# Moving parts of the last layer's bias to ScalarE and dropping one summand from TensorE in a six-layer cross network

## The chip, the cores and the metric

The kernel runs on one core of a Trainium2 chip. The metric is the device time of one execution in microseconds, the median over several executions. The engines that matter here are TensorE (PE in the profile, its weight loads PEld), VectorE (DVE), ScalarE (ACT) and the issuing queues of the transfers (SPq, ACTq). All engines run side by side, each through its own instructions in order, and wait for each other through semaphores.

## The reference

```python
B, F, D, L = 4096, 26, 16, 6
Din = min(F * D, 1024)          # 416
# x0: (4096, 416), ws: (6, 416, 416), bs: (6, 416), all bf16

def reference(x0, ws, bs):
    x = x0
    for l in range(ws.shape[0]):
        x = x0 * (x @ ws[l] + bs[l]) + x
    return x
```

Since every layer multiplies by the same x0, the state can be written x = x0 * c, where c starts at 1 and each layer adds x @ ws[l] + bs[l] to it. The kernel keeps this c, and multiplies it by x0 to get the next layer's input.

## The kernel before

**Layout.** For the layers 0 to 4 everything is transposed: the 416 features lie on the partitions, as three main blocks of 128 (index m) and a remainder of 32, and the 4096 rows of the batch lie along the free axis, as two strips (index s) of 2048 columns, each of four groups of 512. A tile is a pair (s, m). `CM` holds c for the main blocks, `CR` for the remainder (four groups of 32 features stacked on 128 partitions, 512 columns for each strip), `XM0` and `XR[0]` hold x0, `XH` and `XR[1..]` the layer's input and output.

**Layers 1 to 3.** For each tile TensorE forms the product in PSUM in two tiles of 1024 columns (`pt`), ScalarE copies each to SBUF with the bias added (L187), VectorE adds it to c (L188) and multiplies by x0 (L189). The remainder goes through `ew_rem` (L191): ScalarE copies its 512 columns of PSUM in pieces of 256 or 128 columns (L197), then come one add and one multiply on VectorE (L203, L204). The PSUM pool has four tiles of two banks, taken in turn, so TensorE can fill a tile only when ScalarE has copied the one that lay there four tiles earlier.

**The fifth layer, `feeding_layer`** (l = 4), does the same, but it also prepares what the last layer needs of c. The last layer works in rows: its output block of 128 batch rows by 416 features is x0 * (c + b5 + x @ w5), and so c + b5 is wanted in rows. For each of the six tiles A, Bt, C (strip 0, m = 0, 1, 2) and Dt, E, F (strip 1), `rows_out` (L351) adds the last layer's bias to c in place on VectorE (L349), and a transposing transfer on the SP queue turns it into `XLrows` (L232). For strip 1 only the first three of each group's four blocks of 128 columns get the bias; the fourth belongs to the last group of output blocks, whose bias TensorE adds itself (L481). `rem_out` (L378) does the same for the remainder, by way of `scrR` (L380), and `xl_rem` (L307) copies that into `XLrows` on ScalarE (L312). Since the bias is added to c in place, the multiply that makes the last layer's input from c (L345, L376) has to be done before it.

The order of VectorE's work in this layer is written out by hand: `pin` keeps the instructions of an engine in program order. The names in that list are `evict` (ScalarE's copy out of PSUM, L333), `add` (L341), `mul` (L345; with a 4 it takes the four groups, 2048 columns, in one instruction), `rem` (L374, L376), `last_bias` (L349). `layer_products` computes two tiles and calls `between` after the products of the first: there ScalarE evicts that first tile, and for the pair E, F the function `before_last` (L408) puts `xl_rem(0)` ahead of it.

**The last layer** works through eight quads of four output blocks, two quads a round, in four rounds. In a round u counts the eight blocks; each has a PSUM bank. TensorE computes the block (L464 for the main blocks, L477 for the remainder), ScalarE copies it to a tile `t` (L519), VectorE adds `XLrows` (L523), and one step later multiplies by `X0rows` (L505, in `close_product`), and SP issues the transfer to the output (L508). The multiply of a block is queued on VectorE when the next block's add has been queued: add u, multiply u - 1, add u + 1, multiply u, and so on.

In the final round the last three blocks, u = 5, 6 and 7, get their summand c on TensorE instead (`adds`): c's block is multiplied by the identity into the same bank, three products of 128 columns and one of 32 (L468, L470). ScalarE's copies of u = 5 and 6 then need no add on VectorE, and the block u = 7 isn't copied at all: VectorE multiplies it straight out of PSUM (`direct`). The blocks 4 and 5 leave in one transfer, 6 and 7 each in one of its own, the last on ScalarE's queue.

Of the kernel before, what the change touches and what calls it, by code (L numbers as in the profile page):

```python
# [9 lines left out]
ACT = mybir.ActivationFunctionType  # L10
ALU = mybir.AluOpType
# [5 lines left out]
def kernel(  # L17
# [7 lines left out]
    nc = tc.nc  # L25
    B, D = x0.shape
    L = ws.shape[0]
    P = 128
# [5 lines left out]
    CW = 512  # L34
    SW = NG * CW
    NBT = B // P
    LL = L - 1
# [18 lines left out]
    bM = const.tile([P, NK, L], FP32)  # L56
    bR = const.tile([P, L], FP32)
# [9 lines left out]
    CM = big.tile([P, NK, B], BF16, name="CM")  # L67
    CR = big.tile([P, NS * CW], BF16, name="CR")

    def col0(s, g):  # L70
        return SW * s + CW * g
# [8 lines left out]
    def pin(ins):  # L80
        tc.keep_in_program_order(ins)
# [109 lines left out]
    def ew_rem(l, s, pr, nxtR):  # L191
        cols = slice(CW * s, CW * s + CW)
        halves = [slice(a, a + CW // 2) for a in range(0, CW, CW // 2)]
        base = CR[:, cols] if l == 0 else tpool.tile([P, 2 * CW], BF16, name="t")
        n = CW // (4 if l == 2 or l and s else 2)
        for a in range(0, CW, n):
            nc.scalar.activation(base[:, a:a + n], pr[:, a:a + n], ACT.Identity, bias=bR[:, l:l + 1], scale=1.0)  # L197
        if l == 0:
            for a in halves:
                part = slice(CW * s + a.start, CW * s + a.stop)  # L200
                pin(nc.vector.tensor_tensor(out=nxtR[:, part], in0=CR[:, part], in1=XR[0][:, part], op=ALU.mult))
            return
        nc.vector.tensor_tensor(out=CR[:, cols], in0=base[:, 0:CW], in1=CR[:, cols], op=ALU.add)  # L203
        nc.vector.tensor_tensor(out=nxtR[:, cols], in0=CR[:, cols], in1=XR[0][:, cols], op=ALU.mult)  # L204
# [102 lines left out]
    def xl_rem(s):  # L307
        dst = XLrows[:, 16 * s:16 * s + 16, NK * P:D].rearrange("p (g i) r -> p i g r", g=NG)
        src = scrR[s][:].rearrange("p i (g r) -> p i g r", g=NG)
        n = 4 if s else 2  # L310
        for i in range(0, 4, n):
            pin(nc.scalar.copy(dst[:, i:i + n], src[:, i:i + n]))  # L312
# [13 lines left out]
    def feeding_layer(l, cur, curR, nxt, nxtR):  # L326
        tiles = [(s, m) for s in range(NS) for m in range(NK)]
        pts, ts = {}, {}

        def evict(t):  # L330
            for h in range(2):
                ts[t + (h,)] = tpool.tile([P, 2 * CW], BF16, name="t")
                nc.scalar.activation(ts[t + (h,)][:], pts[t][h][:].rearrange("p a b -> p (a b)"), ACT.Identity,  # L333
                                     bias=bM[:, t[1], l:l + 1], scale=1.0)

        def c_of(t, h):
            c0 = col0(t[0], 2 * h)
            return CM[:, t[1], c0:c0 + 2 * CW]

        def add(t, h):  # L340
            pin(nc.vector.tensor_tensor(out=c_of(t, h), in0=ts[t + (h,)][:], in1=c_of(t, h), op=ALU.add))  # L341

        def mul(t, h=0, n=2):
            c0, w = col0(t[0], 2 * h), n * CW
            pin(nc.vector.tensor_tensor(out=nxt[t[0]][:, t[1], 2 * CW * h:2 * CW * h + w], in0=CM[:, t[1], c0:c0 + w],  # L345
                                        in1=XM0[:, t[1], c0:c0 + w], op=ALU.mult))

        def last_bias(c, bias):
            pin(nc.vector.tensor_scalar(out=c, in0=c, scalar1=bias, scalar2=None, op0=ALU.add))  # L349

        def rows_out(t):  # L351
            s, m = t
            c = CM[:, m, SW * s:SW * s + SW]
            if s:
                c = c.rearrange("p (g r) -> p g r", g=NG)[:, :, 0:3 * P]
            last_bias(c, bM[:, m, LL:L])
            xl_dmat(s, m)

        A, Bt, C, Dt, E, F = tiles
        layer_products(l, 0, tiles, pts, cur, curR, evict)  # L360
        evict(Bt)
        pr2 = psum.tile([P, 2, CW], FP32, tag="ps", name="pr2")
        for s in range(NS):
            mm_rem(l, s, pr2[:, s, :], cur, curR)
        tr = []
        for s in range(NS):
            tr.append(tpool.tile([P, 2 * CW], BF16, name="t"))
            for a in range(0, CW, CW // 2):
                nc.scalar.activation(tr[s][:, a:a + CW // 2], pr2[:, s, a:a + CW // 2], ACT.Identity, bias=bR[:, l:l + 1], scale=1.0)

        def rem(s, op):
            part = slice(CW * s, CW * s + CW)
            if op == ALU.add:
                pin(nc.vector.tensor_tensor(out=CR[:, part], in0=tr[s][:, 0:CW], in1=CR[:, part], op=op))  # L374
            else:
                pin(nc.vector.tensor_tensor(out=nxtR[:, part], in0=CR[:, part], in1=XR[0][:, part], op=op))  # L376

        def rem_out(s):  # L378
            last_bias(CR[:, CW * s:CW * s + (3 * P if s else CW)], bR[:, LL:L])
            nc.sync.dma_start_transpose(out=scrR[s][:], in_=CR[:, CW * s:CW * s + CW])  # L380

        add(A, 0)
        mul(A, 0)
        add(A, 1)
        add(Bt, 0)
        mul(A, 1)
        add(Bt, 1)
        rows_out(A)
        rem(0, ALU.add)
        mul(Bt, 0, 4)  # L390
        rem(0, ALU.mult)
        rem(1, ALU.add)
        rem_out(0)
        rows_out(Bt)
        rem(1, ALU.mult)

        layer_products(l, 2, tiles, pts, cur, curR, evict)
        evict(Dt)
        add(C, 0)
        add(C, 1)  # L400
        rem_out(1)
        mul(C, 0, 4)
        add(Dt, 0)
        add(Dt, 1)
        rows_out(C)
        mul(Dt, 0, 4)

        def before_last(t):  # L408
            xl_rem(0)
            evict(t)  # L410

        layer_products(l, 4, tiles, pts, cur, curR, before_last)
        evict(F)
        add(E, 0)
        rows_out(Dt)
        add(E, 1)
        mul(E, 0, 4)
        add(F, 0)
        add(F, 1)
        rows_out(E)  # L420
        mul(F, 0, 4)
        xl_rem(1)
        return lambda: rows_out(F)
# [22 lines left out]
    l = LL  # L446
# [14 lines left out]
    def mm_q_full(q, g, py, closes, adds=False):  # L461
        s, i = quads[q]
        for k in range(NK):
            nc.tensor.matmul(py[:, 0:D], lhsT=q_x(q, g, k), rhs=WM[:, l, k, :],  # L464
                             start=((not closes) and k == 0), stop=(closes and not adds and k == NK - 1))
            if adds:
                c0 = col0(s, g) + 128 * i
                nc.tensor.matmul(py[:, P * k:P * k + P], lhsT=CM[:, k, c0:c0 + 128], rhs=ident[:], start=False, stop=False)  # L468
        if adds:
            nc.tensor.matmul(py[:, NK * P:D], lhsT=CR[:, CW * s + 128 * i:CW * s + 128 * i + 128],  # L470
                             rhs=ident[:, 32 * g:32 * g + 32], start=False, stop=True)
# [59 lines left out]
    for q, at, done in rounds:  # L531
        tiles = [psum.tile([P, 2, CW], FP32, tag="ps", name=f"py{n}") for n in range(4)]
        bank = [tiles[n][:, a, :] for n, a in at]

        final = q + 2 == NQ

        def close(groups):
            u = groups[0][0]
            srcs = [tiles[at[g[0]][0]][:, at[g[0]][1]:at[g[0]][1] + len(g), 0:D] for g in groups]
            if q == 0:  # L540
                evict_quad(u, srcs[0])
                return
            paired = final and u in (0, 1, 4, 5)
            j = u % 2 if paired else 0
            if not j:
                outs.append(opool.tile([P, 2, D], BF16, name="o"))
            ew(q + u // 4, u % 4, srcs, outs[-1], j, bool(j) or not paired, nc.scalar if final and u == 7 else nc.sync,
               final and u >= 5, final and u == 7)

        for u in range(done):  # L550
            if q == 0:
                mm_q_open(q, u, bank[u])
            else:
                mm_q_full(q, u, bank[u], False)
        mm_q_rem(q, bank[0:4], done)
        close([range(done)])
        mm_q_rem(q + 1, bank[4:8], 0)
        for u in range(done, 8):
            mm_q_full(q + u // 4, u % 4, bank[u], True, final and u >= 5)
            if at is ENDS:  # L560
                close([[u]])
            elif u % 2:
                close([[u - 1, u]] if at is PAIRS else [[u - 1], [u]])
                if q == 0 and u == 3:
                    last_rows_out()
# [31 lines left out]
```

## Time and profile before

| | |
|---|---|
| median of 3 runs | 128.79 us (128.64 to 128.90) |
| the profiled execution's own time | 128.94 us |
| its span, first to last instruction | 127.1 us |
| granted TensorE clock, mean | 0.995 |
| busy: PE, DVE, ACT | 122.9, 102.4, 89.0 us |
| rate of the transfers over the span | 129 GB/s |

The profile shows one execution. What lies outside the span (128.94 - 127.1, some 1.8 us) is start and end of the program and is the same for both kernels. Rows of the timeline read: start in us from the span's start, duration, engine, line of the kernel, operation, output and inputs with their shapes, and in brackets the idle time of the engine just ahead and what ended it. A row "x4" stands for four instructions one behind the other, with the time from the start of the first to the end of the last. An instruction's duration includes a part that overlaps the next one on its engine, so in a row of instructions the distance from start to start is shorter than the duration; sums are made with that distance. "L349" is line 349 of the kernel before.

### The profile page before, as it was taken

The page shows a single profiled execution, that of the slowest core. Times are in us where ns is not written, and L with a number is a line of the kernel's source. Part 1 is how long each engine was busy: PE and PEld are TensorE (multiplying, and loading weights), DVE is VectorE, ACT ScalarE, POOL GpSimd, SP SyncE. Part 2 cuts the span into 40 slices and gives each one's busy share as a digit, 9 for nine tenths or more (in the row PEclk, how much of TensorE's full clock was granted, in tenths as well). Part 3 has the DMA queues.
Part 4 walks back from the last instruction along what each step waited for, and adds up shares of the span by engine and source line. Part 5 has one row for each costly group of instructions (what it writes and reads, how often), then busy time and mean ns, then how long its engine had stood idle before and what let it go on. Part 6 is the DMA issues. An engine that isn't in the chain of part 4 may idle for free.

```text
span 127.1 us, 3940 instructions
## 1 busy us (share of the span) xinstructions
PE 122.9 (97%) x1682; PEld 55.2 (43%) x1682; DVE 102.4 (81%) x188; ACT 89.0 (70%) x117; POOL 4.6 (4%) x18
## 2 busy tenths in 40 slices
PE   7999999999999999999999999999999999999990
PEld 3243443453444354435344535443534445455450
DVE  0023679774989898998898998898999999999991
ACT  0137865896869486879495869495859698688770
POOL 4004000310000000000000000000000000000000
PEclk9999999999999999999999999999999999999997
DMA  3999999999990000000000000000039999999975
GB/s 93 245 219 218 164 211 241 220 329 334 337 309 26 0 5 0 8 0 5 0 5 0 5 0 0 5 0 5 0 71 140 204 72 247 186 220 329 286 251 163
DMA packets 42230, 16.38 MB, mean 129 GB/s; under 512 B 31034, under 2 KB 42212, under 8 KB 42212
## 3 DMA queue, kind: packets, MB, share of 16 engines
q1 hardware_dynamic: 37432, 15.40, 54.9%
q10 hardware_dynamic: 4780, 0.72, 3.7%
q8 instruction: 13, 0.21, 0.8%
q14 instruction: 5, 0.04, 0.1%
HBM read 6.15 MB, written 3.41 MB: 75 GB/s over the span
## 4 chain that ended last, share of the span: by engine, by line
PE 68%; DVE 17%; DMA 8%; issue 3%; ACT 1%; DVEq 1%
PE pt L209 40%; PE ph L241 13%; DMA XLrows<-CM 8%; PE wps L148 4%; PE pt L215 4%; PE pr L225 4%; DVE XH L345 4%; DVE CM L341 4%; DVE o L505 3%; DVE t L523 3%; PE ph L248 2%; DVE CM L349 1%; PE pr L221 1%; ACT t L333 1%; DVE CR L374 1%
## 5 line engine op out<-in xcount | busy, mean ns | idle before, releaser
L209 PE MATMUL pt<-XH,WM 128*32 128x512 bf16 x1152 | 65.2, 379 | 0.0
L187 ACT ACTIVATE t<-pt,bM 128x1024 bf16<-128x1024 f32 x36 | 37.2, 1115 | 12.5 <-PE pt L215 12.5
L209 PEld LDWEIGHTS <-WM 128*32 128x32 bf16 x1152 | 29.7, 97 | 33.8 <-issue 5.1
L188 DVE TENSOR_TENSOR CM<-t,CM 128x1024 bf16<-128x1024 bf16 x36 | 24.7, 686 | 4.3 <-ACT t L187 4.3
L189 DVE TENSOR_TENSOR XH<-CM,XM 128x1024 bf16<-128x1024 bf16 x36 | 24.9, 692 | 2.6
L464 PE MATMUL py<-WM,XH 128*128 128x416 bf16 x90 | 17.0, 339 | 0.0
L241 PE MATMUL ph<-XM,WM 128*128 128x512 bf16 x72 | 16.4, 380 | 0.0
L333 ACT ACTIVATE t<-pt,bM 128x1024 bf16<-128x1024 f32 x12 | 12.4, 1115 | 4.1 <-PE pt L215 4.1
L181 ACT ACTIVATE CM<-ph,bM 128x1024 bf16<-128x1024 f32 x12 | 12.5, 1113 | 3.5 <-PE ph L248 3.5
L519 ACT CAST t<-py 128x416 bf16<-128x416 f32 (+1 forms) x18 | 10.8, 602 | 3.2 <-PE py L464 1.4
L183 DVE TENSOR_TENSOR XH<-CM,XM 128x512 bf16<-128x512 bf16 x24 | 8.9, 432 | 4.1 <-ACT CM L181 4.0
L464 PEld LDWEIGHTS <-XH 128*128 128x128 bf16 x90 | 8.5, 98 | 7.5 <-issue 1.2
L241 PEld LDWEIGHTS <-WM 128*128 128x128 bf16 x72 | 6.7, 98 | 8.4 <-issue 1.1
L341 DVE TENSOR_TENSOR CM<-t,CM 128x1024 bf16<-128x1024 bf16 x12 | 8.0, 687 | 0.3 <-ACT t L333 0.3
L345 DVE TENSOR_TENSOR XH<-CM,XM 128x2048 bf16<-128x2048 bf16 (+1 forms) x7 | 7.5, 1068 | 0.2
L215 PE MATMUL pt<-XR,WR 32*128 32x512 bf16 x96 | 7.3, 379 | 0.0
L505 DVE TENSOR_TENSOR o<-t,X0rows 128x832 bf16<-128x832 bf16 (+1 forms) x15 | 7.1, 482 | 0.0
L197 ACT ACTIVATE t<-pr,bR 128x128 bf16<-128x128 f32 (+1 forms) x20 | 5.9, 400 | 1.6 <-PE pr L225 1.6
L225 PE MATMUL pr<-XH,WM 128*32 128x512 bf16 x96 | 6.6, 379 | 0.0
L523 DVE TENSOR_TENSOR t<-t,XLrows 128x832 bf16<-128x832 bf16 (+1 forms) x13 | 6.5, 500 | 0.0
L114 ACT ACT_TABLE_LOAD x1 | 1.3, 1283 | 6.0 <-DMA XM<-in_x_dram 6.0
L157 DVE CAST bM<-pb 128x18 f32<-128x18 bf16 x1 | 0.2, 177 | 5.6 <-PE pb L156 5.6
(64 smaller groups left out, 69.2 us busy)
## 6 DMA issues: line engine op xcount, KB each, us to landing
X0rows<-in_x_dram SPq DMA_DIRECT2D x15, 208.0 KB, 4.9
out_dram<-o SPq DMA_DIRECT2D x10, 208.0 KB, 3.4
WM<-in_ws_dram SPq DMA_DIRECT2D x5, 312.0 KB, 5.8
out_dram<-XH SPq DMA_DIRECT2D x4, 208.0 KB, 3.3
WR<-in_ws_dram SPq DMA_DIRECT2D x4, 130.0 KB, 5.3
WM<-in_ws_dram ACTq DMA_DIRECT2D x1, 312.0 KB, 3.2
out_dram<-o SPq DMA_DIRECT2D x3, 104.0 KB, 1.9
X0rows<-in_x_dram SPq DMA_DIRECT2D x2, 104.0 KB, 5.1
```

The costliest lines, as they stand in the source:

```text
L181: nc.scalar.activation(c, src, ACT.Identity, bias=bias, scale=1.0)
L187: nc.scalar.activation(t[:], src, ACT.Identity, bias=bias, scale=1.0)
L188: nc.vector.tensor_tensor(out=c, in0=t[:], in1=c, op=ALU.add)
L189: nc.vector.tensor_tensor(out=x, in0=c, in1=XM0[:, m, c0:c0 + 2 * CW], op=ALU.mult)
L209: nc.tensor.matmul(pts[g // 2][32 * q:32 * q + 32, g % 2, :], lhsT=WM[:, l, k, 128 * m + 32 * q:128 * m + 32 * q + 32], rhs=cur[s][:, k, C ...
L215: nc.tensor.matmul(pts[g // 2][:, g % 2, :], lhsT=WR[32 * g:32 * g + 32, l, 128 * m:128 * m + 128], rhs=curR[32 * g:32 * g + 32, CW * s:CW ...
L225: nc.tensor.matmul(pr[32 * g:32 * g + 32, :], lhsT=WM[:, l, k, NK * P:D], rhs=cur[s][:, k, CW * g:CW * g + CW], start=False, stop=(k == NK ...
L241: nc.tensor.matmul(pt[:, gl, :], lhsT=WM[:, 0, k, 128 * m:128 * m + 128], rhs=cur[:, k, c0:c0 + CW], start=(k == 0 and not after_row), sto ...
L333: nc.scalar.activation(ts[t + (h,)][:], pts[t][h][:].rearrange("p a b -> p (a b)"), ACT.Identity, bias=bM[:, t[1], l:l + 1], scale=1.0)
L341: pin(nc.vector.tensor_tensor(out=c_of(t, h), in0=ts[t + (h,)][:], in1=c_of(t, h), op=ALU.add))
L345: pin(nc.vector.tensor_tensor(out=nxt[t[0]][:, t[1], 2 * CW * h:2 * CW * h + w], in0=CM[:, t[1], c0:c0 + w], in1=XM0[:, t[1], c0:c0 + w], ...
L464: nc.tensor.matmul(py[:, 0:D], lhsT=q_x(q, g, k), rhs=WM[:, l, k, :], start=((not closes) and k == 0), stop=(closes and not adds and k == ...
```

## The change

Five edits:

- In `ew_rem` the remainder of strip 1 in layer 3 is copied in two pieces of 256 columns instead of four of 128. Layers 1 and 2 stay as they are.
- The last bias of the remainder of strip 0 goes from VectorE to ScalarE (`rem_bias(0)`, 512 columns), and the multiply `rem(0, ALU.mult)` is moved ahead of `mul(Bt, 0, 4)` so that the bias can follow it at once. The bias of strip 1's remainder stays on VectorE, but is moved from behind `add(C, 1)` to ahead of it, with its transfer.
- Of tile C's last bias, ScalarE adds the upper 1024 of 2048 columns (`half_bias`), VectorE the lower 1024 (`rows_out(C, True)`). `half_bias` stands in `before_last`, on ScalarE between `xl_rem(0)` and the eviction of E.
- `rows_out(Dt)` is moved from behind `add(E, 0)` to ahead of it.
- In the final round block 5 gets its summand on VectorE like the blocks before it; TensorE adds it for the blocks 6 and 7 alone.

What is computed is the same.

```diff
@@ -192,7 +192,7 @@
         cols = slice(CW * s, CW * s + CW)
         halves = [slice(a, a + CW // 2) for a in range(0, CW, CW // 2)]
         base = CR[:, cols] if l == 0 else tpool.tile([P, 2 * CW], BF16, name="t")
-        n = CW // (4 if l == 2 or l and s else 2)
+        n = CW // (4 if l == 2 or (s and l == 1) else 2)
         for a in range(0, CW, n):
             nc.scalar.activation(base[:, a:a + n], pr[:, a:a + n], ACT.Identity, bias=bR[:, l:l + 1], scale=1.0)
         if l == 0:
@@ -348,9 +348,14 @@
         def last_bias(c, bias):
             pin(nc.vector.tensor_scalar(out=c, in0=c, scalar1=bias, scalar2=None, op0=ALU.add))
 
-        def rows_out(t):
+        def half_bias(t):
             s, m = t
-            c = CM[:, m, SW * s:SW * s + SW]
+            c = CM[:, m, SW * s + 2 * CW:SW * s + SW]
+            pin(nc.scalar.activation(c, c, ACT.Identity, bias=bM[:, m, LL:L], scale=1.0))
+
+        def rows_out(t, done=False):
+            s, m = t
+            c = CM[:, m, SW * s:SW * s + (2 * CW if done else SW)]
             if s:
                 c = c.rearrange("p (g r) -> p g r", g=NG)[:, :, 0:3 * P]
             last_bias(c, bM[:, m, LL:L])
@@ -375,8 +380,14 @@
             else:
                 pin(nc.vector.tensor_tensor(out=nxtR[:, part], in0=CR[:, part], in1=XR[0][:, part], op=op))
 
+        def rem_bias(s):
+            c = CR[:, CW * s:CW * s + (3 * P if s else CW)]
+            if s:
+                last_bias(c, bR[:, LL:L])
+            else:
+                pin(nc.scalar.activation(c, c, ACT.Identity, bias=bR[:, LL:L], scale=1.0))
+
         def rem_out(s):
-            last_bias(CR[:, CW * s:CW * s + (3 * P if s else CW)], bR[:, LL:L])
             nc.sync.dma_start_transpose(out=scrR[s][:], in_=CR[:, CW * s:CW * s + CW])
 
         add(A, 0)
@@ -387,8 +398,9 @@
         add(Bt, 1)
         rows_out(A)
         rem(0, ALU.add)
+        rem(0, ALU.mult)
+        rem_bias(0)
         mul(Bt, 0, 4)
-        rem(0, ALU.mult)
         rem(1, ALU.add)
         rem_out(0)
         rows_out(Bt)
@@ -397,22 +409,24 @@
         layer_products(l, 2, tiles, pts, cur, curR, evict)
         evict(Dt)
         add(C, 0)
+        rem_bias(1)
+        rem_out(1)
         add(C, 1)
-        rem_out(1)
         mul(C, 0, 4)
         add(Dt, 0)
         add(Dt, 1)
-        rows_out(C)
-        mul(Dt, 0, 4)
 
         def before_last(t):
             xl_rem(0)
+            half_bias(C)
+            rows_out(C, True)
+            mul(Dt, 0, 4)
             evict(t)
 
         layer_products(l, 4, tiles, pts, cur, curR, before_last)
         evict(F)
+        rows_out(Dt)
         add(E, 0)
-        rows_out(Dt)
         add(E, 1)
         mul(E, 0, 4)
         add(F, 0)
@@ -545,7 +559,7 @@
             if not j:
                 outs.append(opool.tile([P, 2, D], BF16, name="o"))
             ew(q + u // 4, u % 4, srcs, outs[-1], j, bool(j) or not paired, nc.scalar if final and u == 7 else nc.sync,
-               final and u >= 5, final and u == 7)
+               final and u >= 6, final and u == 7)
 
         for u in range(done):
             if q == 0:
@@ -556,7 +570,7 @@
         close([range(done)])
         mm_q_rem(q + 1, bank[4:8], 0)
         for u in range(done, 8):
-            mm_q_full(q + u // 4, u % 4, bank[u], True, final and u >= 5)
+            mm_q_full(q + u // 4, u % 4, bank[u], True, final and u >= 6)
             if at is ENDS:
                 close([[u]])
             elif u % 2:
```

## The prediction

> **What bounds the kernel now.** I read the page first: busy times and the chain of waits.
>
> ```profile
> PE 122.9 (97%) x1682; PEld 55.2 (43%) x1682; DVE 102.4 (81%) x188; ACT 89.0 (70%) x117; POOL 4.6 (4%) x18
> ...
> PE 68%; DVE 17%; DMA 8%; issue 3%; ACT 1%; DVEq 1%
> ```
>
> TensorE is never idle between the first products and the last block, so up to there nothing gets faster unless TensorE does less or is stalled less. VectorE has the next share of the chain. So next the waits of VectorE from 86 to 128 us:
>
> ```profile
> DVE CM L341 <- ACT t L333: 0.3, 1, 0.3
> ```
>
> One wait, at the first add of the fifth layer; from there VectorE runs back to back to the end and is the second bound. Then the timeline of the last 8 us; these rows are picked from it:
>
> ```profile
> 119.26 2.46 PE L464 MATMUL py<-WM,XH 128*128 128x416 bf16 x13
> ...
> 121.63 0.51 ACT L519 CAST t<-py 128x416 bf16<-128x416 f32 x1
> 122.11 0.34 PE L464 MATMUL py<-WM,XH 128*128 128x416 bf16 x1
> 122.59 0.36 DVE L505 TENSOR_TENSOR o<-t,X0rows 128x416 bf16<-128x416 bf16 x1
> 123.16 0.36 DVE L505 TENSOR_TENSOR o<-t,X0rows 128x416 bf16<-128x416 bf16 x1
> 123.52 0.18 PE L470 MATMUL py<-ident,CR 128*128 128x32 bf16 x1
> 123.56 0.38 SPq L508 DMA_DIRECT2D out_dram<-o  x1
> 123.84 0.58 DVE L505 TENSOR_TENSOR o<-py,X0rows 128x416 bf16<-128x416 f32 x1
> 124.03 0.42 SPq L508 DMA_DIRECT2D out_dram<-o  x1
> 124.46 0.38 ACTq L508 DMA_DIRECT2D out_dram<-o  x1
> ```
>
> The thirteenth of the first row's products, at 119.26 + 2.46 - 0.34 = 121.38, is the first of block 5, and 122.11 the first of block 6. 122.59 is the multiply of block 3, 123.16 that of block 5, 123.84 that of block 7. The transfer of blocks 4 and 5 is issued at 123.56, as soon as block 5's multiply ends (123.52); those of 6 and 7 follow. Last, the transfers in stretches (the last two columns are the busy share of the transfer engines and GB/s):
>
> ```profile
> 124.20:124.50 0.30, 0.00 (x0) 0.00 (x0) 0.23 (x1) 0.00 (x0) 0.00 (x0) 1.00 0.17 47
> 124.50:125.80 1.30, 0.00 (x0) 0.00 (x0) 0.00 (x0) 0.00 (x0) 0.00 (x0) 0.98 0.96 312
> ```
>
> After a gap comes one full burst, 1.30 x 312 = 406 KB, which is the last three transfers (208, 104 and 104 KB). So the end is set by the burst, and the burst begins with the transfer of blocks 4 and 5: it is released by block 5's multiply, some 0.95 us ahead of it (123.56 to 124.50). Block 7 by itself would end almost as late: 124.46 + 0.95 + 0.33 for its 104 KB is 125.74.
>
> **The change part by part.** *Final round.* TensorE loses block 5's four small products. Block 5 took 122.11 - 121.38 = 0.73; its three products of 416 columns alone take 0.53 (twelve take from 119.26 to 121.38, 0.177 each). So TensorE ends 0.20 earlier: block 7 is complete at 123.52 + 0.18 - 0.20 = 123.50. But VectorE gets an add, and it is queued ahead of the multiplies of blocks 4 to 7. Multiplies of 416 columns follow each other by 0.285 (122.59 to 123.16 is two of them). Without any help from layer five: multiply 3 at 122.59, add 5 at 122.88, multiply 4 at 123.16, 5 at 123.45, 6 at 123.73, 7 at 124.02: block 5 is 0.29 later than before, block 7 0.18. TensorE's 0.20 doesn't help, since multiply 7 waits for multiply 6 on VectorE. Had VectorE all the lead one can wish for, add 5 would still wait for its copy: ScalarE is busy with block 4 until 121.63 + 0.53, so the copy ends at 122.67 and add 5 begins at 122.69; then multiply 5 is at 123.26 (+0.10) and multiply 7 at 123.83 (-0.01).
>
> *How much lead there can be.* In rounds three and four VectorE follows ScalarE's copies closely:
>
> ```profile
> 118.20 0.51 ACT L519 CAST t<-py 128x416 bf16<-128x416 f32 x1
> 118.80 0.58 DVE L523 TENSOR_TENSOR t<-t,XLrows 128x832 bf16<-128x832 bf16 x1
> ```
>
> This copy ends at 118.71 and could release the add some 0.03 later (the hand-over from block 5's multiply to its issue, 123.52 to 123.56, is of that size), at 118.74: a lead of 0.06 at most passes here. The copies are paced by TensorE, which doesn't change before block 5. So whatever layer five saves, at most 0.06 reaches the final round.
>
> *VectorE in layer five.* Rows for the bias, for the wait between dependent instructions and for the gate at E:
>
> ```profile
> 88.53 0.69 DVE L341 TENSOR_TENSOR CM<-t,CM 128x1024 bf16<-128x1024 bf16 x1 [0.29 <-ACT t L333]
> 89.33 0.69 DVE L345 TENSOR_TENSOR XH<-CM,XM 128x1024 bf16<-128x1024 bf16 x1
> ...
> 95.16 0.35 DVE L349 TENSOR_SCALAR CR<-CR,bR 128x512 bf16<-128x512 bf16 x1
> 95.42 0.75 DVE L349 TENSOR_SCALAR CM<-CM,bM 128x2048 bf16<-128x2048 bf16 x1
> 96.08 0.42 DVE L376 TENSOR_TENSOR XR<-CR,XR 128x512 bf16<-128x512 bf16 x1
> ...
> 102.68 0.61 DVE L349 TENSOR_SCALAR CM<-CM,bM 128x1536 bf16<-128x1536 bf16 x1
> 103.21 0.68 DVE L341 TENSOR_TENSOR CM<-t,CM 128x1024 bf16<-128x1024 bf16 x1
> ```
>
> Saved: the remainder's bias, 0.26 (95.16 to 95.42), and half of C's, 0.66 - 0.40 = 0.26 (2048 columns take 0.66, 1536 take 0.53, so 1024 take 0.40). Given back: a multiply directly behind the add that it needs begins 0.11 after its end (89.33 against 88.53 + 0.69), where independent ones overlap by 0.08, so each such neighbourhood costs 0.19. The new order makes two, `rem(0)` add and multiply, and `add(C, 1)` and `mul(C)`; `mul(Dt)` with the bias behind it may be a third. 0.52 - 0.38 = 0.14, with the third -0.05. Against that, before, VectorE also waited some 0.08 for C's second copy ahead of `add(C, 1)`, which the later arrival takes in. I take a lead of about 0.1 at `add(E, 1)`, between -0.05 and 0.27, where the copy of E's second half stops it (one step of 1.0 behind the first half, as the four evictions from 100.78 to 103.79 below show: 101.78 + 1.12 + 0.03 = 102.93 against 103.21). Either way the lead that counts is 0.06; only at the low end does it turn into 0.05 of delay.
>
> *ScalarE in layer five.* This is where the change could hurt TensorE:
>
> ```profile
> 94.95 4.13 ACT L333 ACTIVATE t<-pt,bM 128x1024 bf16<-128x1024 f32 x4 [1.33 <-PE pt L215]
> ...
> 99.36 0.40 ACT L312 COPY XLrows<-scrR 128x256 bf16<-128x256 bf16 x1
> ...
> 100.78 1.11 ACT L333 ACTIVATE t<-pt,bM 128x1024 bf16<-128x1024 f32 x1 [1.03 <-PE pt L215]
> ...
> 103.79 1.12 ACT L333 ACTIVATE t<-pt,bM 128x1024 bf16<-128x1024 f32 x1
> 104.79 0.63 ACT L312 COPY XLrows<-scrR 128x512 bf16<-128x512 bf16 x1
> ```
>
> `rem_bias(0)` (0.63 by the copy of 512 columns) follows `rem(0)`'s multiply, done by 93.95, and fits ahead of 94.95 into 1.33 of idle time: nothing. `half_bias` falls into the 1.03 of idle time ahead of E. Copies in SBUF cost 0.40 for 256 columns and 0.63 for 512, so 1024 take about 1.09, 1.0 to the next start. ScalarE is free at 99.36 + 0.31 = 99.67; `mul(C)`, which has to have read C, ends by 99.2 as now. So ScalarE is ready for E at 100.67, 0.11 before TensorE delivers E at 100.78. I take 0 and keep 0.2 as the dear end (no overlap with its neighbours, and 0.1 more since no row shows this form). That cover is thin, and behind it there is none:
>
> ```profile
> 104.65 0.66 PE L477 MATMUL py<-WR,XR 32*128 32x416 bf16 x8
> ...
> 109.57 0.53 PE L477 MATMUL py<-WR,XR 32*128 32x416 bf16 x8
> ```
>
> The same eight products take 0.13 longer in the first round than in the second: the last two need the bank of F's second half, which ScalarE leaves at 103.79 + 1.12 = 104.91. TensorE already waits for this chain of four evictions, so each 0.1 by which E starts late is 0.1 at the end.
>
> The Trainium skill speaks against this placement: ScalarE: Activation LUTs, section Rules for kernel authors, says to put an add on VectorE, up to about 3x faster per element in bf16. The rows agree, 0.40 on VectorE against about 1.0 on ScalarE. By that rule the sum would be the price of the second rival below; by the rows it is 0 as long as the idle time holds it.
>
> *Transfers of layer five.* SP's order is the same.
>
> ```profile
> 95.57 1.73 SPq L380 DMA_TRANSPOSE scrR<-CR  x1
> ```
>
> Strip 0's remainder, with its bias ready at 94.6, can be issued ahead of the 95.57 of now, which brings `xl_rem(0)` forward if anything; C's needs both halves of its bias, VectorE's near 100.7 and ScalarE's near 100.8, no later than now; Dt's comes one add, 0.6, earlier. VectorE waits for none of them now (its only wait stands above). Worth 0.
>
> *Layer 3's copy in two pieces* saves ScalarE two instructions, but the wait of 0.29 ahead of 88.53 shows that VectorE begins layer five at the pace of TensorE's products and ScalarE's evictions: nothing of it passes.
>
> **Sum.** Block 5's multiply comes at 123.45 - 0.06 = 123.39 instead of 123.16, +0.23, and with it the burst; block 7's by 0.12, which stays inside. TensorE and ScalarE add 0. The profiled execution of 128.94 becomes 129.17. It lies 0.15 above the median of the runs, so the median becomes 128.79 + 0.23, about 129.02. A measurement of this kernel tells about 0.2% (0.26 us) from no change; the forecast, +0.18%, lies just inside. Its own bounds are +0.10 (unlimited lead) and +0.34 (0.05 of delay).
>
> **Rivals.** *The tail isn't set by the burst but by block 7's multiply.* For it: block 7's own transfer would end only 0.1 before the burst does. Against it: the burst has no gap in 1.30 us. Then the shift is 0.12 less up to 0.13 of lead, 128.78 to 128.91, no change.
>
> *`half_bias` makes E late, and TensorE stalls* (slower). It decides as soon as ScalarE is ready for E later than 100.78, that is if `half_bias` starts later than 99.78 or takes over 1.11 to the next start. For it: 0.11 of cover on an operation no row shows in this form, and the banks of F with no slack. Against it: the remainder's transfer comes earlier, and `mul(C)` is long done. At the dear end 0.20 of stall, and the tail's 0.23 on top: 129.22, +0.33%.
>
> *TensorE's saving reaches the end* (faster): if the last multiply followed block 7's products alone, 0.20 less, 128.59; with the stall of 0.13 at F's bank gone too, 128.46. Against it: VectorE's order, add 5 ahead of four multiplies, and E's eviction being released by TensorE itself, so that ScalarE can't be earlier.
>
> **How the numbers follow.** The forecast has 0.58, of which 0.38 lie within 0.2% and 0.20 above; the tail set by block 7 0.10; the late E 0.25, all slower; TensorE's saving 0.07. Faster 0.07, within 0.2% 0.48, slower 0.45. The range goes from 128.75, just under the case of block 7, to 129.32, which takes in the dear end of E with 0.1 of the forecast's own spread.
>
> **What would show it.** In the changed kernel: block 5's last product about 0.2 earlier, yet its add on VectorE at about 122.8 with four multiplies behind it and the last at 123.96; the issue of blocks 4 and 5 near 123.78; the burst's end at about 126.0 instead of 125.8. ScalarE's idle time before E should be under 0.2, with E at 100.78, and the eight L477 still 0.66. It is wrong if E starts later than 100.8, if VectorE idles before block 5's add, or if the burst begins at 124.5 as before.

## The result, and the profile after

The changed kernel takes 129.03 us (median of 18 runs, 128.77 to 129.37), the kernel before beside it 128.69 (18 runs, 128.49 to 128.99): ratio 1.0027, 95% interval [1.0019, 1.0035], that is 0.34 us slower [0.24, 0.45]. The forecast was 129.02 and +0.23. That the two absolute times agree to 0.01 is luck: the forecast started from 128.79 for the kernel before, which took 128.69 here, and this difference of 0.10 hides nearly all of the 0.11 by which the slowdown was forecast too small.

The two profiled executions don't reach the fifth layer at the same time. That alone tells nothing of the change: other kernels below, whose first 88 us are those of before, lie 0.4 us apart there. To compare the traces I measure from VectorE's first add of the fifth layer (the origin, below), which stands at 88.53 before and at 88.30 here. In times from there the end of the span is at 38.60 before (127.13 - 88.53) and 38.91 now, +0.30 before rounding. The spans themselves, 127.1 and 127.2 us, hide that. What the change does ahead of the fifth layer (layer 3's copies) doesn't show in these times; the run `layer5_only` below has it in its total.

The page of the changed kernel (busy times, chain by engine; PE has 1678 instructions instead of 1682, and the chain's share of DVE went from 17% to 25%):

```profile
PE 122.6 (96%) x1678; PEld 55.0 (43%) x1678; DVE 102.4 (81%) x188; ACT 90.4 (71%) x117; POOL 4.9 (4%) x18
...
PE 68%; DVE 25%; issue 3%; ACT 1%; DVEq 0%
```

Rows of its timeline, from the start of the fifth layer, the gate in the fourth round, and the end:

```profile
88.30 0.69 DVE L341 TENSOR_TENSOR CM<-t,CM 128x1024 bf16<-128x1024 bf16 x1 [0.30 <-ACT t L333]
...
118.57 0.59 DVE L537 TENSOR_TENSOR t<-t,XLrows 128x832 bf16<-128x832 bf16 x1
...
121.98 0.51 ACT L533 CAST t<-py 128x416 bf16<-128x416 f32 x1
...
122.66 0.37 DVE L537 TENSOR_TENSOR t<-t,XLrows 128x416 bf16<-128x416 bf16 x1
...
123.16 0.18 PE L484 MATMUL py<-ident,CR 128*128 128x32 bf16 x1
123.23 0.37 DVE L519 TENSOR_TENSOR o<-t,X0rows 128x416 bf16<-128x416 bf16 x1
123.62 0.38 SPq L522 DMA_DIRECT2D out_dram<-o  x1
123.80 0.58 DVE L519 TENSOR_TENSOR o<-py,X0rows 128x416 bf16<-128x416 f32 x1
...
124.41 0.38 ACTq L522 DMA_DIRECT2D out_dram<-o  x1
```

121.98 is ScalarE's copy of block 5. It ends at 122.49, but VectorE, which does things in order, comes to block 5's add only at 122.66, and then does four multiplies without a pause: 4, 5 (123.23), 6, 7 (123.80). TensorE had finished at 123.34 and waits for nobody any more. In times from the fifth layer's start:

| | before | after | shift |
|---|---|---|---|
| TensorE's last product ends | 35.17 | 35.04 | -0.13 |
| block 5's multiply | 34.64 | 34.93 | +0.30 |
| issue of blocks 4 and 5 | 35.03 | 35.33 | +0.30 |
| block 7's multiply | 35.32 | 35.50 | +0.19 |
| issue of block 7 | 35.93 | 36.11 | +0.18 |
| end of the span | 38.60 | 38.91 | +0.30 |

The end moved by what block 5's multiply moved, and not by what block 7's did. That the two agree to 0.01 is chance: in three traces whose blocks 4 and 5 are issued at 35.02 to 35.04 (before, `layer5_only`, `no_summand5`) the span ends anywhere from 38.6 to 38.8. The argument rests on the medians below. The transfers of the changed kernel in the gap ahead of the last burst (last columns: busy share, GB/s):

```profile
124.00:124.40 0.40, 0.00 (x0) 0.00 (x0) 0.38 (x1) 0.00 (x0) 0.00 (x0) 1.00 0.03 8
```

That gap has become wider (before, 0.17 of the time was busy from 124.20 to 124.50; now nothing moves for most of 124.00 to 124.40, though the whole execution runs 0.23 ahead): block 3's transfer is over and that of blocks 4 and 5 hasn't begun.

In layer five, ScalarE and TensorE of the changed kernel:

```profile
99.38 1.17 ACT L354 ACTIVATE CM<-CM,bM 128x1024 bf16<-128x1024 bf16 x1
100.12 0.40 PE L215 MATMUL pt<-XR,WR 32*128 32x512 bf16 x4
100.61 1.11 ACT L333 ACTIVATE t<-pt,bM 128x1024 bf16<-128x1024 f32 x1
...
104.42 0.72 PE L491 MATMUL py<-WR,XR 32*128 32x416 bf16 x8
```

and the same products of TensorE for E before:

```profile
100.35 0.40 PE L215 MATMUL pt<-XR,WR 32*128 32x512 bf16 x4
```

The last products for E end at 100.52 now and ended at 100.75 before. E's eviction begins 0.09 behind them now and began 0.03 behind them then (100.78): 0.06 late. The eight remainder products, which wait for F's bank at the end of the four evictions, take 0.72 instead of 0.66: TensorE has these 0.06 as a stall.

### The profile page after: what moved, and what is told of

Its sections match the earlier page's. It is cut to its first block, busy times and chain, and to the rows that moved or that the text cites. A ratio compares the mean times of both kernels' runs of the same rounds, so it can differ in the third digit from the quotient of the medians.

```text
span 127.2 us, 3931 instructions
## 1 busy us (share of the span) xinstructions
PE 122.6 (96%) x1678; PEld 55.0 (43%) x1678; DVE 102.4 (81%) x188; ACT 90.4 (71%) x117; POOL 4.9 (4%) x18
## 4 chain that ended last, share of the span: by engine, by line
PE 68%; DVE 25%; issue 3%; ACT 1%; DVEq 0%
PE pt L209 39%; PE ph L241 13%; DVE XH L345 6%; DVE CM L341 5%; DVE t L537 5%; PE wps L148 4%; DVE o L519 4%; PE pt L215 4%; PE pr L225 4%; DVE CM L349 2%; DVE XH L519 1%; PE ph L248 1%; PE pr L221 1%; ACT t L333 1%; DVE XR L381 1%
## 5 line engine op out<-in xcount | busy, mean ns | idle before, releaser
L333 ACT ACTIVATE t<-pt,bM 128x1024 bf16<-128x1024 f32 x12 | 12.4, 1115 | 2.1 <-PE pt L215 2.1
```

## The experiments

Times are medians beside the kernel before on the same chip; in brackets the ratio and its 95% interval.

### Which part costs the time

`tail_only`, from the kernel before:

```diff
-               final and u >= 5, final and u == 7)
+               final and u >= 6, final and u == 7)
...
-            mm_q_full(q + u // 4, u % 4, bank[u], True, final and u >= 5)
+            mm_q_full(q + u // 4, u % 4, bank[u], True, final and u >= 6)
```

> The kernel before, with only the final round changed (block 5's summand added by VectorE). Theory of the added instruction: VectorE has no lead, so block 5's multiply comes 0.29 us later than before and the last burst of transfers with it: +0.29 us against before. Rival, layer five's new hand-overs on ScalarE cost the time: about 0. Rival, TensorE's 0.20 is worth something once layer five is left alone: below 0.

Measured: 129.06 against 128.65 (1.0029 [1.0018, 1.0041]).

```profile
88.39 0.69 DVE L341 TENSOR_TENSOR CM<-t,CM 128x1024 bf16<-128x1024 bf16 x1 [0.29 <-ACT t L333]
123.70 0.89 SPq L508 DMA_DIRECT2D out_dram<-o  x2
```

The first of these two issues is that of blocks 4 and 5: 123.70 - 88.39 = 35.31, against 35.03 before, +0.28. The final round alone makes the whole slowdown, of the size that the theory gave.

`layer5_only`, from the changed kernel, takes the same two lines back to `u >= 5`.

> The changed kernel with the final round as before (TensorE adds block 5's summand). Theory of the added instruction: layer five's part changes nearly nothing, E's eviction 0.06 late, that is 0.06 of stall of TensorE, but block 5's multiply stays where it was: 0 to +0.06 us against before. Rival, half_bias is the cost: +0.2 or more. Rival, VectorE's relief in layer five is worth time by itself: -0.1.

Measured: 128.69 against 128.65 (1.0004 [0.9995, 1.0012]). The issue of blocks 4 and 5 is where it was (123.28 - 88.24 = 35.04). This kernel has layer 3's copies in two pieces as well as the new layer five, so the four edits outside the final round together cost nothing that shows. The eight remainder products show that TensorE's 0.06 of stall belongs to this part:

```profile
88.24 0.69 DVE L341 TENSOR_TENSOR CM<-t,CM 128x1024 bf16<-128x1024 bf16 x1 [0.29 <-ACT t L333]
104.36 0.72 PE L491 MATMUL py<-WR,XR 32*128 32x416 bf16 x8
123.28 0.89 SPq L522 DMA_DIRECT2D out_dram<-o  x2
```

`no_summand5` changes only the second of the two lines, so that neither engine adds block 5's summand:

```diff
-            mm_q_full(q + u // 4, u % 4, bank[u], True, final and u >= 5)
+            mm_q_full(q + u // 4, u % 4, bank[u], True, final and u >= 6)
```

> The kernel before, with block 5's summand left out altogether: neither TensorE nor VectorE adds c to it, so TensorE's 0.20 us is saved and VectorE gets nothing more to do. Theory that the end follows block 5's multiply on VectorE: that multiply stays where it was, so 0 us against before (within 0.05), with block 7's multiply 0.1 earlier. Rival, TensorE's saving reaches the end once VectorE doesn't pay for it: -0.2 us.

Measured: 128.70 against 128.65 (1.0003 [0.9993, 1.0013]).

```profile
88.16 0.69 DVE L341 TENSOR_TENSOR CM<-t,CM 128x1024 bf16<-128x1024 bf16 x1 [0.30 <-ACT t L333]
123.18 0.89 SPq L508 DMA_DIRECT2D out_dram<-o  x2
123.97 0.38 ACTq L508 DMA_DIRECT2D out_dram<-o  x1
```

Blocks 4 and 5 are issued at 35.02 as before, block 7 at 35.81, 0.12 earlier, and the time doesn't fall (the interval is -0.09 to +0.17). TensorE's saving is worth nothing that shows by itself; between this kernel and `tail_only` lies one add on VectorE, and that is the loss.

### The place of the add

Two kernels add one instruction to the kernel before and change nothing else:

```diff
+    spare = big.tile([P, D], BF16, name="spare")
...
         close_product()
         pending.append((tv, q, g0, n, o, j, last, eng))
+        if q == NQ - 1 and g0 == 2:
+            pin(nc.vector.tensor_tensor(out=spare[:], in0=X0rows[:, 0, :], in1=X0rows[:, 1, :], op=ALU.add))
```

This is `add_behind_5`; in `add_ahead_of_4` the condition is `g0 == 1`, and the two lines stand ahead of `close_product()`.

> The kernel before with one more add of 416 columns on VectorE (two rows of X0rows into a tile that nobody reads), queued where the change queues block 5's add: ahead of the multiply of block 4. TensorE does all that it did. Theory: the place of one instruction on VectorE is the whole price, +0.29 us against before (0.25 to 0.4). Rival, something else of the change costs the time: under 0.1.

> The same additional add on VectorE, queued behind the multiply of block 5 instead. Theory that the last burst of transfers, released by block 5's multiply, sets the end, with block 7's own transfer 0.06 to 0.1 us behind it: blocks 6 and 7 come 0.18 later, the burst begins where it did: +0.05 to +0.12 us against before. Rival, the number of instructions ahead of block 7's multiply sets the end wherever they stand: the same as with the add ahead of block 4, +0.29.

Measured: ahead of 4, 128.93 against 128.72 (1.0015 [1.0003, 1.0028], +0.04 to +0.36 us); behind 5, 128.74 (1.0000 [0.9988, 1.0012]). First the one, then the other:

```profile
88.48 0.69 DVE L342 TENSOR_TENSOR CM<-t,CM 128x1024 bf16<-128x1024 bf16 x1 [0.29 <-ACT t L334]
123.79 0.89 SPq L509 DMA_DIRECT2D out_dram<-o  x2
124.58 0.38 ACTq L509 DMA_DIRECT2D out_dram<-o  x1
```

```profile
88.27 0.69 DVE L342 TENSOR_TENSOR CM<-t,CM 128x1024 bf16<-128x1024 bf16 x1 [0.29 <-ACT t L334]
123.30 0.90 SPq L509 DMA_DIRECT2D out_dram<-o  x2
124.37 0.38 ACTq L509 DMA_DIRECT2D out_dram<-o  x1
```

Block 7 is issued at 36.10 in both, 0.17 later than before. Blocks 4 and 5 are issued at 35.31 in the first and at 35.03 in the second. The first takes 0.19 longer than the second. So block 7's multiply doesn't make that difference; the transfer of blocks 4 and 5, and with it block 5's multiply, does. (Block 6's issue moves along, since it stands behind that transfer on SP; the pair doesn't tell the two apart.)

Against before, both came out below what was expected: +0.20 instead of 0.25 to 0.4, and 0.00 instead of 0.05 to 0.12, though the issues are where they were expected. The traces show a difference that the expectations hadn't: in these two kernels the last burst runs faster. The first stretch is of `add_ahead_of_4`, the second of the changed kernel (0.8 us from about the burst's start on, GB/s last):

```profile
124.75:125.55 0.80, 0.00 (x0) 0.00 (x0) 0.00 (x0) 0.00 (x0) 0.00 (x0) 1.00 1.06 351
```

```profile
124.55:125.35 0.80, 0.00 (x0) 0.00 (x0) 0.00 (x0) 0.00 (x0) 0.00 (x0) 1.00 0.98 309
```

`add_behind_5` has 348 there, and the ten traces without the additional tile of 416 columns (those of the two kernels with a split transfer left aside) have 306 to 321. At 351 instead of 312 the burst's 406 KB take an estimated 0.14 less. Why it runs faster isn't shown. So the two are to be compared with each other; that block 7's delay would cost nothing in the kernel before is not shown by `add_behind_5` alone.

### Taking the two blocks' transfer apart

```diff
-            paired = final and u in (0, 1, 4, 5)
+            paired = final and u in (0, 1)
```

> The changed kernel, blocks 4 and 5 leaving in a transfer each. Theory that the end is set by the burst which begins with the joint transfer of blocks 4 and 5: block 4 can leave 0.25 us earlier, the end then follows block 7's own transfer: 0.15 to 0.23 us faster than the changed kernel, so +0.1 to +0.2 us against before. Rival, block 7's multiply already sets the end: as the changed kernel, +0.34 us.

> The kernel before, blocks 4 and 5 leaving in a transfer each. Theory of the burst: block 4 leaves about 0.28 us earlier, then block 7's own transfer sets the end, which lies only 0.06 to 0.1 us ahead of the present one: -0.06 to -0.1 us. Rival, block 7's multiply already sets the end: 0.

Both expectations missed: 129.08 (1.0033 [1.0020, 1.0045]) from the changed kernel, and 129.16 (1.0038 [1.0024, 1.0051]) from the kernel before. The first lies near where its rival put it, the second where neither did. The second's rows, and a stretch of its transfers:

```profile
88.29 0.69 DVE L341 TENSOR_TENSOR CM<-t,CM 128x1024 bf16<-128x1024 bf16 x1 [0.29 <-ACT t L333]
123.18 1.39 SPq L508 DMA_DIRECT2D out_dram<-o  x3
124.17 0.40 SPq L508 DMA_DIRECT2D out_dram<-o  x1
```

```profile
124.90:125.20 0.30, 0.00 (x0) 0.00 (x0) 0.00 (x0) 0.00 (x0) 0.00 (x0) 1.00 0.41 128
```

Block 4 does leave earlier (34.89 from the origin), but SP needs 0.4 to 0.5 for each issue, so the three transfers of blocks 4, 5 and 6 are issued half a microsecond apart and block 6's slides from 35.50 to 35.88. The burst breaks up (0.41 busy from 124.90 to 125.20) and ends later. The test brought in an issue of its own, and so tells nothing for or against the burst; what it shows is that SP has hardly a pause left here. The two kernels of the section above are the cleaner test.

### E's eviction

`e_late`, from the changed kernel:

```diff
+    spare = big.tile([P, 256], BF16, name="spare")
...
             half_bias(C)
+            pin(nc.scalar.copy(spare[:], XM0[:, 0, 0:256]))
             rows_out(C, True)
```

> The changed kernel with one more copy of 256 columns on ScalarE (its result used by nobody) between half_bias and E's eviction, 0.31 us to the next start. Theory that TensorE waits for the chain of four evictions: all 0.31 comes out at the end, +0.6 us against before (0.55 to 0.7). Rival, there is slack behind E: as the changed kernel, +0.34.

Measured: 129.15 against 128.65 (1.0041 [1.0027, 1.0055]), +0.53 [0.35, 0.71] where the changed kernel has +0.34.

```profile
99.24 1.17 ACT L355 ACTIVATE CM<-CM,bM 128x1024 bf16<-128x1024 bf16 x1
100.29 0.41 ACT L423 COPY spare<-XM 128x256 bf16<-128x256 bf16 x1
100.58 1.13 ACT L334 ACTIVATE t<-pt,bM 128x1024 bf16<-128x1024 f32 x1
...
104.28 0.85 PE L493 MATMUL py<-WR,XR 32*128 32x416 bf16 x8
```

From half_bias to the next instruction it is 1.05, so in the changed kernel ScalarE was free for E at 99.38 + 1.05 = 100.43, while E was ready at 100.55 (100.52 and the 0.03 of before). The additional copy of 0.29 used up that cover first: E stands at 100.58 - 88.16 = 12.42 from the origin instead of 12.31, 0.11 later. The eight products take 0.13 longer than the changed kernel's. Blocks 4 and 5 are issued at 123.62 - 88.16 = 35.46, also 0.13 later than in the changed kernel. So in the trace the coupling is as expected, delay for delay, and the 0.31 of the expectation was wrong by the cover and the 0.06 that were already there. The measured times agree with that, but their intervals overlap and don't give the size by themselves.

That raises the question what made E 0.06 late, since ScalarE was free in time. `l5_no_half`, from `layer5_only`:

```diff
-            half_bias(C)
-            rows_out(C, True)
+            rows_out(C)
```

> The changed kernel's layer five without half_bias (VectorE adds the bias to all of C), the final round as before. Theory that half_bias costs E its 0.06 by the order of the waits, not by its length: E's eviction stands 0.04 behind TensorE's last product for it, as before, the eight remainder products take 0.66 again, and the time is that of before (-0.05 to +0.05 us). Rival, E's 0.06 has another reason: E and the eight products as in the changed kernel.

```profile
88.15 0.69 DVE L341 TENSOR_TENSOR CM<-t,CM 128x1024 bf16<-128x1024 bf16 x1 [0.29 <-ACT t L333]
100.47 1.11 ACT L333 ACTIVATE t<-pt,bM 128x1024 bf16<-128x1024 f32 x1 [0.82 <-PE pt L215]
123.34 0.38 SPq L521 DMA_DIRECT2D out_dram<-o  x1
```

Measured: 128.87 against 128.72 (1.0008 [0.9996, 1.0020]). ScalarE stood idle for 0.82 ahead of E, and E is still at 12.32, and the eight products still take 0.72. So it isn't half_bias, and the expectation missed. VectorE, with all of C's bias to do, now is late: blocks 4 and 5 are issued at 35.19, +0.16. The relief that half_bias brings is real, it only has nowhere to go but to cover the detours of the new order.

`after_t8` is the changed kernel with `bufs=8` for `tpool`.

> The changed kernel with eight buffers instead of six for ScalarE's copies. If E's eviction is 0.06 late since it also waits for ScalarE's own earlier copy into the same buffer, the deeper pool takes that wait away: E 0.06 earlier, 0.05 us less than the changed kernel, +0.29 against before. Rival, the second wait stays with any number of buffers: as the changed kernel, +0.34.

Measured: 129.13 (1.0033 [1.0022, 1.0044]), with E where it was (88.23 and 100.55, 12.32). So the number of buffers isn't the reason.

What the trace has of E in the changed kernel, by the view of line L333 around it:

```profile
L333 ACTq EVENT_SEMAPHORE  x1: 17/17/17, 100.5 to 100.5; - x1
L333 ACT ACTIVATE t<-pt,bM x1: 1115/1115/1115, 100.6 to 100.6; 128x1024 bf16<-128x1024 f32 x1
```

ScalarE's queue does a wait of its own ahead of the eviction, just when TensorE is done; before, no such instruction stood there, and the two of the view came after the eviction's start. In the trace's record of semaphores, E's eviction waited for TensorE alone before; now it waits for TensorE, in that separate instruction, and for earlier work of ScalarE itself. The same holds from C's first eviction on, which follows `rem_bias(0)` and stands ahead of half_bias:

```profile
94.77 1.11 ACT L333 ACTIVATE t<-pt,bM 128x1024 bf16<-128x1024 f32 x1 [0.35 <-PE pt L215]
```

That is 6.47 from the origin, against 94.95 - 88.53 = 6.42 before, late like E's. All kernels with `rem_bias(0)` on ScalarE have E at 12.31 or 12.32, all others at 12.25 (`e_late` aside). My reading is that with this instruction on ScalarE the evictions have a second thing to wait for, and TensorE's signal is taken by the separate wait, which costs 0.06. But these kernels have the rest of layer five's new order and layer 3's copies in common too, and none was run with `rem_bias(0)` alone, so the cause stays a reading.

### Taking TensorE's stall away

In `before_rem_late` (from the kernel before) and `l5_rem_late` (from `layer5_only`):

```diff
-        mm_q_rem(q + 1, bank[4:8], 0)
+        if q:
+            mm_q_rem(q + 1, bank[4:8], 0)
         for u in range(done, 8):
+            if q == 0 and u == 3:
+                mm_q_rem(q + 1, bank[4:8], 0)
```

> The kernel before, with the eight products of the remainder in the last layer's first round split: the second four (into the banks that F's eviction frees) moved behind the third block's products, so that TensorE needn't wait for F's eviction. Theory: TensorE gains 0.12, but VectorE, back to back since layer five, has no lead: 0 us against before (within 0.05). Rival, TensorE alone is the bound: -0.12 us.

> The changed kernel's layer five, the final round as before, and the second four remainder products moved behind the third block's as in the run before. Theory: layer five gives VectorE a lead of 0.12 that was lost to TensorE's pace and to E's late eviction; with that stall gone both engines are 0.12 earlier to the end: -0.08 to -0.12 us against before. Rival, layer five's part brings nothing: +0.05 as without the move.

Measured, against 128.65: 128.68 (1.0005 [0.9996, 1.0013]) and 128.64 (1.0002 [0.9993, 1.0011]). The second should have been faster. `before_rem_late` shows why neither tells anything:

```profile
104.69 0.35 PE L477 MATMUL py<-WR,XR 32*128 32x416 bf16 x4
...
105.61 0.35 PE L477 MATMUL py<-WR,XR 32*128 32x416 bf16 x4
105.90 0.35 PE L464 MATMUL py<-WM,XH 128*128 128x416 bf16 x1
```

From the first remainder product to the first of the next block it is 1.21 (105.90 - 104.69); before, the same work took 1.13, from 104.65 to

```profile
105.78 0.34 PE L464 MATMUL py<-WM,XH 128*128 128x416 bf16 x1
```

Going over to the 32-row products and back once more costs more than the stall it avoids: about 0.29 passes from the last four of them to the next product. TensorE gained nothing, so whether a gain of TensorE's here would pass is open. No kernel of the study beats the one before by more than the measurement can tell.

## Why the prediction was right

**What bounds the end: right.** The last 8 us are VectorE's list, and the end follows block 5's multiply by way of the burst. `tail_only`, `no_summand5` and the pair of additional adds show it from both sides. In `no_summand5` block 7's transfer is issued 0.12 earlier and nothing is gained that shows; in the pair it is issued at the same time, and the kernel whose blocks 4 and 5 are issued 0.28 later is 0.19 slower. Over the other kernels, too, the time goes with the issue of blocks 4 and 5, within the intervals: 0.01 later and +0.05 us in `layer5_only`, 0.16 and +0.10 in `l5_no_half`, 0.28 and +0.38 in `tail_only`, 0.30 and +0.34 in the changed kernel, 0.43 and +0.53 in `e_late`. The rival of block 7's multiply falls with that, and so does the one of TensorE's saving.

**The price of the add: right.** The sum had 0.29 without help from layer five; `tail_only` moved the issue by 0.28.

**The lead from layer five: mechanism right, size off.** VectorE's second add of E is at 102.86 - 88.30 = 14.56 from the origin, and was at 103.21 - 88.53 = 14.68: a lead of 0.12 where I took 0.1.

```profile
102.86 0.69 DVE L341 TENSOR_TENSOR CM<-t,CM 128x1024 bf16<-128x1024 bf16 x1
```

It then had to pass the copies of rounds three and four. The step that failed is the sentence "Either way the lead that counts is 0.06": that gate moved too. Shortly ahead of the gate the lead was still 0.10 (28.17 from the origin for the first of these rows, 28.27 for its match before, at 116.80); the second row is the copy that sets the gate:

```profile
116.47 0.58 DVE L537 TENSOR_TENSOR t<-t,XLrows 128x832 bf16<-128x832 bf16 x1
...
118.03 0.51 ACT L533 CAST t<-py 128x416 bf16<-128x416 f32 x1
```

The copy is at 29.73 from the origin and was at 118.20 - 88.53 = 29.67. With E 0.06 late and TensorE stalled by as much, TensorE's blocks and ScalarE's copies come 0.06 later. The copy ends at 118.54 and releases the add 0.03 later, as the prediction reckoned, but that is at 118.57 - 88.30 = 30.27, where the add was before (118.80 - 88.53). So block 5's multiply moved by 0.30 and not by 0.23. That is the term that was mis-sized, by 0.06 of the 0.11 by which +0.34 exceeds +0.23; the rest lies within the interval. The root of it is the same 0.06 that the sum put at nothing in "TensorE and ScalarE add 0".

**ScalarE in layer five: half right.** The cover of 0.11 ahead of E was there (0.12 by `e_late`), and the length of the add cost nothing: 1.05 on ScalarE against 0.40 on VectorE, close to what the rows gave, and hidden. The rule of the Trainium skill (ScalarE: Activation LUTs, section Rules for kernel authors) to put an add on VectorE agrees with these two lengths. But the second rival, E late and TensorE stalled, did come true by 0.06, by a way that wasn't among its conditions: half_bias started and ended in time. Two of the signs that the prediction named went against it. "E starts later than 100.8" did happen (100.8 is 12.27 from the origin, E is at 12.31), and the eight products aren't at 0.66 but at 0.72.

**Layer 3, the transfers, TensorE's 0.20: right.** VectorE's only wait of the last 40 us is still the one at the first add of layer five, 0.30 long, so the transfers of layer five hold nothing up, and with layer 3's pieces in it `layer5_only` takes what the kernel before takes. TensorE's last product ends 0.20 earlier in `tail_only`, as reckoned, and 0.13 earlier in the changed kernel, where the stall of 0.06 is taken off.

**The chances.** The sum fell just inside 0.2%, the measurement (+0.27% [0.19, 0.35]) just outside. With the 0.06 in the sum the likeliest case would have been slower.

## What to carry to other kernels

When two engines are both full to the end, taking work from one and giving less of it to the other is judged by the order on the receiving engine: the price is what is queued behind the new instruction up to the one that releases the last transfers, and an instruction two places further back can cost less or nothing. A saving made earlier reaches the end only through every gate between, and a gate that is set by a third engine moves when that engine is touched. Compare two traces from a common event, not from their starts, when the difference sought is smaller than what the loading phase varies.

## What the runs showed of the hardware that was not expected

A dependent pair of neighbours in VectorE's list costs as in the kernel before (an add of C and the multiply behind it are 0.8 apart, at 96.93 and 97.72 of the changed kernel, against 0.60 for the two adds of E at 102.26 and 102.86, which don't need each other), so the order of a list counts as well as its length. E's eviction with a separate wait ahead of it begins 0.09 behind TensorE's last product instead of 0.03. SP's issues of outputs came 0.4 to 0.5 apart in `before_split45`, where two small transfers in the place of one, with a third waiting behind them, made the kernel 0.5 slower. The last burst ran at 351 and 348 GB/s in the two kernels with an additional tile of 416 columns, at 306 to 321 in the ten without it and with the joint transfer; the reason is open.
